# Loading plain attention units with three DMAs for both batches, and running them first

## The chip, the cores and the metric

The kernel runs on one core of a Trainium2 chip. A core has a matrix engine (TensorE, PE in the profile, with its weight loads as PEld), a vector engine (VectorE, DVE), a scalar engine (ScalarE, ACT), GpSimd (POOL) and SyncE (SP). Each engine follows its own list of instructions in order and waits on semaphores for the others. Transfers between the chip's main memory and the on-chip memory run on 16 DMA engines that all issuers share. In this kernel GpSimd issues all loads of q, k, v and nearly all weight loads; SyncE issues two early loads and all stores.

The metric is the device time of one execution in microseconds (us). The kernel before takes 175.22 us (median of 3 runs, 174.65 to 175.56).

## The reference

Attention over 8 batches, 8 heads, 576 positions and 64 dimensions, with two kinds of mask: the first four heads ("plain") look back over 32 neighbouring positions, the last four ("dilated") over 128 positions, every fourth of them. Its output, put together per token (4608 tokens x 512), goes through a soft mixture of experts: 8 experts with 4 slots each.

```python
mask_plain = (rel >= 0) & (rel < window)                      # window 32
mask_dil = (rel >= 0) & (rel < window * dilation) & (rel % dilation == 0)
scores = np.where(masks, scale * q @ k.T, -1e9)
attn = softmax(scores) @ v                                    # per batch and head
x = attn.transpose(0, 2, 1, 3).reshape(B * S, H * D)

logits = x @ phi                                              # 4608 x 32
d = softmax(logits, axis=0);  c = softmax(logits, axis=1)
slot_input = (d.T @ x).reshape(E, S_per_e, D)
slot_out[e] = np.maximum(slot_input[e] @ w1[e], 0) @ w2[e]    # w1: 512 x 1024, w2: 1024 x 512
out = c @ slot_out
```

The inputs are float32: 28.3 MB of q, k and v, 33.6 MB of weights. The output is 9.4 MB. The kernel converts to bfloat16 inside the loads.

## The kernel before

**Units.** Attention is cut into eight units, `u` = 0 to 7. A unit is one kind of head (four heads) of one pair of batches, `bp = u // 2`. `kind(u)` is 0 for plain and 1 for dilated; before the change it is `1 - u % 2`, so the units run dilated, plain, dilated, plain and so on.

**Loading a unit** (`load_unit`, L435 to L452). The stage `stg` has three slots of 96 rows by 9216 bfloat16; unit `u` uses slot `u % 3`. Rows 0 to 31 hold q, 32 to 63 k, 64 to 95 v. In the source a head has 8 stretches of 72 positions; a stretch, 72 x 64 = 4608 elements, is one row of half a slot. A dilated unit is loaded by three DMAs (one each for q, k, v), in which a row holds two neighbouring stretches. A plain unit is loaded by six: one for each of q, k, v and each batch of the pair. Batches alternate by row, and the two halves of a row are two heads (16 stretches apart). Each DMA is issued on GpSimd.

**Copies on GpSimd** (`interleave`, L598 to L610; `blocked`, L583). In a plain unit the two halves of a row must come to lie side by side before a transpose can take both. GpSimd does this with eight copies per unit, two for each of four parts `j`, viewing pairs of bfloat16 as one float32. The first part goes to scratch `hTT`, the others into slots of the stage that earlier copies have read. Dilated units need no copies.

**Stages of a unit.** `st_T` (L625) transposes a unit's 96 rows on TensorE in four parts and ScalarE writes the results to `TT` (L667), two neighbouring columns packed as one 32-bit word. `st_S` computes scores on TensorE (L685), ScalarE takes the exponential into `PT` (L692), VectorE multiplies by the mask (L700): six blocks per unit. `st_V` transposes v back (L710) and VectorE copies it to `VN` (L715): four groups. `st_P` multiplies `PT` by `VN` (L739); VectorE takes reciprocals of the sums (L748) and writes the scaled outputs to a buffer `XB` (L750): four groups. `XB` is one of five buffers, one for a batch and kind. Before the change a group's output belongs to one batch (`b = 2 * bp + bpar`), and a buffer is taken at the first of the two groups of a batch. `st_X` transposes `XB` (L767) into `XT` (L779, L780). After both kinds of a pair of batches, `st_L` computes logits (L794), their exponentials (L799), and adds the slots' inputs into `psA` (L838).

**Weights and the end.** Weight loads go out on GpSimd too (L481, L495, L870), between the unit loads, into a buffer `WD`, then into slots of the stage and into `TT` as units are done with them. After attention come the first layer of all experts (L950), the second (L1025), and the output matmuls (L1092, L1143), whose results ScalarE and VectorE scale (L1066, L1067, L1109) and SyncE stores (L1055 to L1058). The last weights arrive as two column halves, and the outputs' first part is computed and stored by halves too, so that stores of the first half go out while the second half's weights are under way. Filler matmuls (L1161) are placed in a stretch given by `FILL`.

**Order.** The order of instructions on each engine is decided before the kernel is built by a small planner, `schedule`: a list scheduler with a cost for each operation, and a key for each, from `due(u, x)` with the constants in `DUE` (a unit's pace, and offsets of each stage) and a tolerance `TOL`. GpSimd's and SyncE's operations keep the order of the program. For GpSimd that order is: unit 0's load, a constant, unit 1's load, the masks, unit 2's load; then for each unit `u`, after the transposes of `u`: weight loads, the load of unit `u + 3` into the slot that `u` has left, and the copies for unit `u + 1` if it is plain:

```python
        if u + 1 < NU and blocked(u + 1):
            interleave(u + 1)
```

The functions that the diff touches follow.

Of the kernel before, what the change touches and what calls it, by code (L numbers as in the profile page):

```python
# [18 lines left out]
SCALE = 1.0 / (D ** 0.5)  # L19
TOL, LINE, FETCH0 = 0.0806, 6.2, 193  # L20
DUE = {"pace": 8.24, "T": -11.42, "Tj": 4.19, "Te": 18.27, "S": -11.29, "Si": 0.41,
       "m": 22.09, "V": 3.07, "Vg": 3.25, "P": 6.98, "Pg": 3.6, "X": 19.47, "Xb": -72.44,
       "L": 4.86, "Lb": 20.25, "x": -24.07}
CT = 72
NU = 8
QB = 96
HALO = 32
# [29 lines left out]
class Op:  # L57
    n = 0
# [269 lines left out]
def bass_dilated_sliding_attn__then__soft_moe_slots_kernel(  # L328
# [23 lines left out]
    VNt = [sb(f"VN{i}", [128, 6, 2, 66]) for i in range(NVN)]  # L352
    XBt = [sb(f"XB{i}", [QB, 6, 256]) for i in range(NXB)]
    XTt = [sb(f"XT{i}", [128, 2, S]) for i in range(NXT)]
# [5 lines left out]
    id0 = sb("id0", [128, 128])  # L360
    ident = sb("ident", [128, 128])
    sel = sb("sel", [128, N_SLOTS])
    fold = sb("fold", [128, N_SLOTS], F32)
# [56 lines left out]
    b_mask = [Buf(), Buf()]  # L420
    b_id0, b_id, b_sel, b_fold, b_rowm, b_phist, b_phi = [Buf() for _ in range(7)]
    b_acc, b_psA, b_csum, b_rcs, b_rtok = [Buf() for _ in range(5)]
# [6 lines left out]
    def kind(u):  # L429
        return 1 - u % 2  # L430

    def load_unit(u):
        bp, ty, s = u // 2, kind(u), u % 3

        def f(g):  # L435
            res = []
            for t, src in enumerate((q, k, v)):
                if ty:
                    rows = src[2 * bp:2 * bp + 2].rearrange(
                        "b h (p c) d -> b (h p) (c d)", c=CT)[:, 32:64]  # L440
                    res.append(g.dma_start(
                        stg[32 * t:32 * t + 32, s, :],
                        rows.rearrange("b (r x) f -> r b (x f)", x=2)))
                    continue
                for bpar in range(2):
                    rows = src[2 * bp + bpar].rearrange(
                        "h (p c) d -> (h p) (c d)", c=CT)[32 * ty:32 * ty + 32]
                    res.append(g.dma_start(  # L448
                        stg[32 * t + bpar:32 * t + 32:2, s, :].rearrange("r (x f) -> r x f", x=2),
                        rows.rearrange("(x r) f -> r x f", x=2)))  # L450
            return res
        op("pool", f, w=[b_stg[s]], cost=3.5, sem=s_u[s], nbytes=96 * 2 * 4608 * 4, ndma=3 if ty else 6)  # L452

# [108 lines left out]
    for j in range(4):  # L562
        op("dve", lambda g, j=j: g.memset(rowm[32 * j:32 * j + 8, :], 1.0), w=[b_rowm], cost=0.1)
        op("dve", lambda g, j=j: g.tensor_copy(sel[32 * j:32 * j + 32, 8 * j:8 * j + 8],
                                               ident[32 * j:32 * j + 32, 32 * j:32 * j + 8]),
           r=[b_id], w=[b_sel], cost=0.1, key=1)
        op("dve", lambda g, j=j: g.tensor_copy(fold[32 * j:32 * j + 32, :],
                                               ident[32 * j:32 * j + 32, 32 * j:32 * j + 32]),
           r=[b_id], w=[b_fold], cost=0.1, key=1)
    op("dve", lambda g: g.memset(phi_pad[:], 0.0), w=[b_phi], cost=0.4, key=1)  # L570
    for hi in range(2):
# [10 lines left out]

    def blocked(u):  # L583
        return u > 0 and kind(u) == 0

# [3 lines left out]
    def il_ap(u, j, y):  # L589
        s_ = u % 3  # L590
        if j == 0:
            ap = hTT[0:96, 1152 * y:1152 * y + 1152]
# [5 lines left out]
    def interleave(u):  # L598
        s_ = u % 3
        for j in range(4):  # L600
            b_il[u, j] = Buf()
            for y in range(2):
                def f(g, j=j, y=y):
# [5 lines left out]
                op("pool", f, r=[b_stg[s_]], a=[b_il[u, j]],  # L609
                   **({"w": [b_scr]} if j == 0 and y == 0 else {}), cost=0.8, port=True)  # L610

# [13 lines left out]
    def st_T(u, j):  # L625
# [5 lines left out]
        def pe(t):  # L631
            for a in range(2):
                for kk in range(9):
                    if blocked(u):
                        i_ = t.transpose(bankb2(pt, a)[:, 96 * kk:96 * kk + 96],  # L635
                                         il_ap(u, j, a)[:, 128 * kk:128 * kk + 128],
                                         ident[0:96, 0:96])
                        continue
                    if ty:
                        c = 36 * (j // 2) + 2 * (9 * a + kk) + j % 2  # L640
                        i_ = t.transpose(bankb2(pt, a)[:, 96 * kk:96 * kk + 96],  # L641
                                         two[:, c, :], ident[0:96, 0:96])
                        continue
                    c = 18 * j + 9 * a + kk
                    for hx in range(2):
                        i_ = t.transpose(
                            bankb2(pt, a)[64 * hx:64 * hx + 64, 96 * kk:96 * kk + 96],
                            src[:, hx, c, :], ident[0:96, 0:96])
            return i_
        o = op("pe", pe, r=[b_id, b_stg[s]] +  # L650
               ([b_il[u, j]] + [b_scr] * (j == 0) if blocked(u) else []), w=[pt], alloc=[pt],
               cost=0.86 if ty == 0 and not blocked(u) else 0.75,
               mode="h" if ty == 0 and not blocked(u) else "f", n=36 if ty == 0 and not blocked(u) else 18,
               key=due(u, DUE["T"] + DUE["Tj"] * j))
# [65 lines left out]
    def st_P(u, g):  # L720
        bp, ty = u // 2, kind(u)
        bpar, h01 = g // 2, g % 2
        b = 2 * bp + bpar
        po, rv = tile(psum, 2), tile(pRV)
        vn = U[u]["v", g]
        al = [po]
        if h01 == 0:
            XB[b, ty] = tile(pXB)
            al.append(XB[b, ty])
        xb = XB[b, ty]  # L730
        pts = {(6 * g + m) // 4: U[u]["p", (6 * g + m) // 4] for m in range(6)}

        def pe(t):
            for m in range(6):
                i, x = divmod(6 * g + m, 4)
                for half in range(2):
                    o_ = 384 * half + QB * x
                    bk, po_ = (half, m) if ty == 0 else (m // 3, 3 * half + m % 3)
                    i_ = t.matmul(pair(po)[:, bk, 65 * po_:65 * po_ + 65],  # L739
# [3 lines left out]
        k0 = due(u, DUE["P"] + DUE["Pg"] * g)  # L743
        op("pe", pe, r=list(pts.values()) + [vn], w=[po], alloc=al, cost=0.46, n=12, key=k0)

        def pv():
            return pair(po)[0:QB, :, 0:390].rearrange("p x (m d) -> p x m d", d=65)
        op("dve", lambda dv: dv.reciprocal(sbt(rv)[:], pv()[:, :, :, 64]),  # L748
           r=[po], w=[rv], alloc=[rv], cost=0.15, key=k0 + 1.0)
        op("dve", lambda dv: dv.tensor_tensor(  # L750
            sbt(xb)[:].rearrange("p m (x h d) -> p h x m d", x=2, h=2)[:, h01], pv()[:, :, :, 0:64],
            sbt(rv)[:].unsqueeze(3).to_broadcast([QB, 2, 6, 64]), AluOp.mult),
           r=[po, rv], **{"w" if h01 == 0 else "a": [xb]}, cost=0.87, key=k0 + 1.2)

# [101 lines left out]
    def wpair(na, nb, s_, steps):  # L856
# [4 lines left out]
        for n, st in enumerate(steps):  # L861
# [11 lines left out]
            for b in bs:  # L873
                b.parts.append((0, 8, 0, 512, pb))
                b.ready.append(o)

    W_AFTER = {2: ["w10"], 3: ["w11"], 4: ["w12"], 5: ["w13"], 6: ["w14"]}
    for u in range(NU):
# [334 lines left out]
```

## Time and profile before

| what | value |
|---|---|
| median of 3 runs | 175.22 us (174.65 to 175.56) |
| the profiled execution | 174.82 us |
| its span, first to last instruction | 173.6 us |
| mean granted TensorE clock | 0.935 |
| PE / PEld / DVE / ACT / POOL busy | 127.1 / 98.5 / 115.3 / 94.9 / 64.3 us |
| read from main memory / written | 61.93 MB / 9.44 MB |

The profile is of one execution. Its page lists busy times of each engine; the span cut in 40 slices with busy shares in tenths (9 is 90% or more), for the DMA engines too; DMA queues; the chain of work that ended last; and the costliest groups of instructions, each with its line, engine, operation, what it writes and reads, and the idle time of the engine just before it with the engine that ended it. "L448" is line 448 of the kernel. DMA engines' shares can pass 1.00 in a short window, since a packet's time is put down as a whole. GB/s counts bytes as written: a load that converts float32 to bfloat16 reads twice as many.

### The profile page before, as it was taken

To read this page: it belongs to the slowest core of one execution; us is meant where nothing else is said; L and a number is where in the kernel's file an instruction comes from. 1 tells how busy PE (TensorE), PEld (TensorE's weight loads), DVE (VectorE), ACT (ScalarE), POOL (GpSimd) and SP (SyncE) were. 2 spreads that over 40 slices of the span, in tenths; PEclk is the share of its full clock that TensorE was granted. 3 is DMA by queue.
4 is the path that set the end of the run, shared out by engine and by line. 5 is a ranking of instruction groups with operands and counts; after the bars stand their busy time and mean duration, and the time that the engine had idled before them with its cause. 6 is when DMAs were issued, how large, how long until landed. Compare 5 with 4: busy or idle time off the path is not lost.

```text
span 173.6 us, 5093 instructions
## 1 busy us (share of the span) xinstructions
PE 127.1 (73%) x2235; PEld 98.5 (57%) x2235; DVE 115.3 (66%) x261; ACT 94.9 (55%) x145; POOL 64.3 (37%) x106
## 2 busy tenths in 40 slices
PE   0004968987889799999898789898759987699000
PEld 0004848976779588788687579576545443452000
DVE  6960059578996989978979996899540110589400
ACT  2310682878878586788788578576400110589200
POOL 7950099330696205980101762935920000000000
PEclk9999985899999999999999999999995699999955
DMA  5999999999999999999999999999999999999997
GB/s 166 286 208 193 210 232 200 215 214 216 237 208 195 216 218 210 233 220 194 215 212 219 215 215 215 215 215 217 219 204 200 212 191 197 272 382 413 436 463 311
DMA packets 10357, 41.28 MB, mean 238 GB/s; under 512 B 2016, under 2 KB 5856, under 8 KB 7008
## 3 DMA queue, kind: packets, MB, share of 16 engines
q0 software_dynamic: 7952, 30.41, 87.2%
q1 hardware_dynamic: 2384, 10.55, 15.4%
q8 instruction: 17, 0.28, 0.6%
q14 instruction: 4, 0.03, 0.0%
HBM read 61.93 MB, written 9.44 MB: 411 GB/s over the span
## 4 chain that ended last, share of the span: by engine, by line
PE 35%; DVE 24%; DMA 22%; ACT 6%; POOL 4%; issue 3%
DMA TT<-in_moe_w_dram 15%; PE ps L641 8%; DMA stg<-in_v_dram 7%; PE ps L635 7%; DVE XB L750 6%; PE ps L710 5%; DVE PT L700 5%; PE ps L685 4%; DVE WD L1066 4%; PE ps L739 3%; PE ps L794 3%; POOL TT L481 3%; PE ps L767 3%; ACT PT L692 3%; ACT TT L667 2%
## 5 line engine op out<-in xcount | busy, mean ns | idle before, releaser
L692 ACT ACTIVATE PT<-ps 128x768 bf16<-128x768 f32 x48 | 37.1, 815 | 13.1 <-PE ps L685 13.0
L667 ACT ACTIVATE TT<-ps 128x864 f32<-128x864 f32 x32 | 27.7, 898 | 17.6 <-PE ps L641 11.9
L750 DVE TENSOR_TENSOR XB<-ps,RV 96x768 bf16<-96x768 f32 x32 | 30.1, 946 | 0.5
L641 PE MATMUL ps<-ident,stg 96*128 96x96 bf16 x288 | 16.5, 224 | 15.9 <-DMA stg<-in_v_dram 15.6
L715 DVE COPY VN<-ps 128x768 bf16<-128x768 bf16 x32 | 17.1, 541 | 13.8 <-PE ps L710 13.5
L641 PEld LDWEIGHTS ps<-ident,stg 96*128 96x128 bf16 x288 | 15.3, 109 | 16.6 <-DMA stg<-in_v_dram 15.6
L739 PE MATMUL ps<-VN,PT 128*128 128x65 bf16 x384 | 17.8, 197 | 3.1 <-issue 1.4
L685 PE MATMUL ps<-TT 64*128 64x96 bf16 x384 | 15.8, 206 | 5.7 <-ACT PT L692 2.3
L710 PE MATMUL ps<-ident,TT 128*128 128x128 bf16 x192 | 16.8, 229 | 1.3 <-issue 0.6
L608 POOL COPY stg<-stg 96x576 f32<-96x576 f32 x24 | 16.8, 698 | 1.5
L739 PEld LDWEIGHTS ps<-VN,PT 128*128 128x128 bf16 x384 | 14.9, 100 | 4.1 <-issue 2.2
L685 PEld LDWEIGHTS ps<-TT 64*128 64x128 bf16 x384 | 9.7, 95 | 10.2 <-ACT PT L692 3.9
L700 DVE TENSOR_TENSOR PT<-PT,mask_d 128x768 bf16<-128x768 bf16 x24 | 15.4, 674 | 0.0
L1067 ACT ACTIVATE WD<-ps,rtok 128x256 f32<-128x256 f32 (+1 forms) x20 | 9.4, 600 | 10.2 <-PE ps L1092 10.2
L448 POOL DMA_DIRECT2D stg<-in_q_dram x8 | 4.1, 518 | 28.4 <-PE ps L641 28.4
L710 PEld LDWEIGHTS ps<-ident,TT 128*128 128x128 bf16 x192 | 11.7, 102 | 4.8 <-issue 1.3
L767 PE MATMUL ps<-ident,XB 96*128 96x96 bf16 x192 | 11.2, 207 | 1.9 <-DVE XB L750 1.6
L700 DVE TENSOR_TENSOR PT<-PT,mask_p 128x768 bf16<-128x768 bf16 x24 | 12.4, 543 | 0.1
L767 PEld LDWEIGHTS ps<-ident,XB 96*128 96x128 bf16 x192 | 9.0, 98 | 3.2 <-DVE XB L750 2.8
L780 ACT ACTIVATE XT<-ps 128x576 bf16<-128x576 bf16 x16 | 9.9, 651 | 1.8 <-PE ps L767 1.7
L635 PE MATMUL ps<-ident,stg 96*128 96x96 bf16 x216 | 10.7, 209 | 0.0
L635 PEld LDWEIGHTS ps<-ident,stg 96*128 96x128 bf16 x216 | 10.0, 99 | 0.5 <-ACT PT L692 0.2
(96 smaller groups left out, 206.5 us busy)
## 6 DMA issues: line engine op xcount, KB each, us to landing
WD<-in_moe_w_dram POOLq DMA_DIRECT2D x4, 1024.0 KB, 23.1
stg<-in_moe_w_dram POOLq DMA_DIRECT2D x3, 1024.0 KB, 29.1
out_dram<-WD SPq DMA_DIRECT2D x1, 3072.0 KB, 11.0
stg<-in_q_dram POOLq DMA_DIRECT2D x4, 576.0 KB, 17.0
stg<-in_k_dram POOLq DMA_DIRECT2D x4, 576.0 KB, 19.1
stg<-in_v_dram POOLq DMA_DIRECT2D x4, 576.0 KB, 21.5
stg<-in_q_dram POOLq DMA_DIRECT2D x8, 288.0 KB, 16.3
stg<-in_k_dram POOLq DMA_DIRECT2D x8, 288.0 KB, 18.0
```

Of the source, the lines that this page charges most:

```text
L608: return g.tensor_copy(o_, i_)
L635: i_ = t.transpose(bankb2(pt, a)[:, 96 * kk:96 * kk + 96], il_ap(u, j, a)[:, 128 * kk:128 * kk + 128], ident[0:96, 0:96])
L641: i_ = t.transpose(bankb2(pt, a)[:, 96 * kk:96 * kk + 96], two[:, c, :], ident[0:96, 0:96])
L667: return ac.activation(d, sv, ACTF.Copy)
L685: i_ = t.matmul(pair(sc)[:, hx, QB * x:QB * x + QB], win(u, 1, h01, blk_, bpar)[64 * hx:64 * hx + 64], win(u, 0, h01, blk_, bpar)[64 * hx: ...
L692: op("act", lambda ac: ac.activation(sbt(pt)[:, 0:768].rearrange("p (x n) -> p x n", x=2), pair(sc)[:, :, 0:384], ACTF.Exp, scale=SCALE), ...
L700: return dv.tensor_tensor(p_, p_, m.unsqueeze(1).to_broadcast([128, 2, 384]), AluOp.mult)
L710: i_ = t.transpose(bankb(pv)[:, 128 * m:128 * m + 128], win(u, 2, h01, m, bpar), ident[:, :])
L715: op("dve", lambda dv: dv.tensor_copy(sbt(vn)[:, :, :, 0:64], bankb(pv)[:, 0:768].rearrange("p (m x d) -> p m x d", m=6, x=2)), r=[pv], w= ...
L739: i_ = t.matmul(pair(po)[:, bk, 65 * po_:65 * po_ + 65], sbt(pts[i])[:, o_:o_ + 128], sbt(vn)[:, m, half, 0:65], start=True, stop=True)
L750: op("dve", lambda dv: dv.tensor_tensor(sbt(xb)[:].rearrange("p m (x h d) -> p h x m d", x=2, h=2)[:, h01], pv()[:, :, :, 0:64], sbt(rv)[: ...
L767: i_ = t.transpose(bankb(px)[:, QB * m:QB * m + QB], sbt(xb)[:, m, 128 * x:128 * x + 128], ident[0:QB, 0:QB])
```

## The change

The change alters how plain units are loaded and what follows from that, and the order of kinds.

- `kind(u)` becomes `u % 2`: units run plain, dilated, plain, dilated.
- A plain unit is loaded by three DMAs, one each for q, k and v. Each writes every third row (`t`, `t + 3`, ...), and the two halves of a row are now the same stretch of the two batches.
- After the copies, side by side lie the two batches, so a transpose puts one batch in partitions 0 to 63 and the other in 64 to 127. The rows are brought to the order that the later stages expect by transposing with a permutation, `perm`, in place of the identity. `perm` is built by one VectorE copy from `ident`. The two columns in a 32-bit word of `TT` are now two heads.
- A group of `st_P` of a plain unit now gives one head of each batch, so it writes two `XB` buffers with one instruction; both are taken at the first group, and the groups are kept in order. For this the five buffers become one tensor, `XBa`, and the two batches' halves of the matmul result are put in the order of the buffers' places.
- `J0` says from which part on a plain unit goes through GpSimd's copies, for the first unit and for the others. It is `(0, 0)`: unit 0, now plain, is copied whole like the others. `interleave(0)` stands before the loop, behind the loads of units 0, 1 and 2. Unit 7, now dilated, has no copies.
- `TOL` and the constants in `DUE` get new values.

```diff
-TOL, LINE, FETCH0 = 0.0806, 6.2, 193
-DUE = {"pace": 8.24, "T": -11.42, "Tj": 4.19, "Te": 18.27, "S": -11.29, "Si": 0.41,
...
+TOL, LINE, FETCH0 = 0.1176, 6.2, 193
+DUE = {"pace": 7.91, "T": -8.23, "Tj": 4.2, "Te": 0.05, "S": -27.93, "Si": 5.43,
...
+J0 = (0, 0)
...
-    XBt = [sb(f"XB{i}", [QB, 6, 256]) for i in range(NXB)]
+    XBa = sb("XB", [QB, NXB, 6, 256])
+    XBt = [XBa[:, i] for i in range(NXB)]
...
     def kind(u):
-        return 1 - u % 2
+        return u % 2
...
             for t, src in enumerate((q, k, v)):
+                rows = src[2 * bp:2 * bp + 2].rearrange("b h (p c) d -> b (h p) (c d)", c=CT)
                 if ty:
...
-                for bpar in range(2):
-                    rows = src[2 * bp + bpar].rearrange(
-                        "h (p c) d -> (h p) (c d)", c=CT)[32 * ty:32 * ty + 32]
+                else:
                     res.append(g.dma_start(
-                        stg[32 * t + bpar:32 * t + 32:2, s, :].rearrange("r (x f) -> r x f", x=2),
-                        rows.rearrange("(x r) f -> r x f", x=2)))
+                        stg[t:96:3, s, :].rearrange("r (b f) -> r b f", b=2),
+                        rows[:, 0:32].rearrange("b r f -> r b f")))
...
+    op("dve", lambda g: g.tensor_copy(
+        perm[:].rearrange("p (t r x) -> p t r x", t=3, x=2),
+        ident[0:96, 0:96].rearrange("p (x r t) -> p t r x", t=3, x=2)),
+       r=[b_id], w=[b_perm], cost=0.2, key=1)
...
-    def blocked(u):
-        return u > 0 and kind(u) == 0
+    def blocked(u, j=3):
+        return kind(u) == 0 and j >= J0[u > 0]
...
     def interleave(u):
         s_ = u % 3
-        for j in range(4):
+        for j in range(J0[u > 0], 4):
...
+                    elif blocked(u, j):
+                        in_, id_ = il_ap(u, j, a)[:, 128 * kk:128 * kk + 128], perm[:]
...
     def st_P(u, g):
...
-        b = 2 * bp + bpar
+        bs = [2 * bp + bpar] if ty else [2 * bp, 2 * bp + 1]
+        first = h01 == 0 if ty else g == 0
...
+        if first:
+            for b in bs:
+                XB[b, ty] = tile(pXB)
+                al.append(XB[b, ty])
...
-                    bk, po_ = (half, m) if ty == 0 else (m // 3, 3 * half + m % 3)
+                    bk, po_ = (half ^ (xi()[0] > xi()[1]), m) if ty == 0 else (m // 3, 3 * half + m % 3)
...
+        o = op("pe", pe, r=list(pts.values()) + [vn], w=[po], alloc=al, cost=0.46, n=12, key=k0,
+               after=[] if first else U[u]["o", bs[0]])
...
+            lo, hi = sorted(xi())
+            c = 128 * bpar + 64 * h01
+            return XBa[:, lo:hi + 1:hi - lo, :, c:c + 64]
...
+    interleave(0)
     W_AFTER = {2: ["w10"], 3: ["w11"], 4: ["w12"], 5: ["w13"], 6: ["w14"]}
```

## The prediction

> **What bounds the kernel now.** I read four views: the page's slices and queues, the landings of single loads, the waits, and the last 50 us in order of time.
>
> The page comes first: engines, slices, queues.
>
> ```profile
> span 173.6 us, 5093 instructions
> PE 127.1 (73%) x2235; PEld 98.5 (57%) x2235; DVE 115.3 (66%) x261; ACT 94.9 (55%) x145; POOL 64.3 (37%) x106
> ...
> DMA  5999999999999999999999999999999999999997
> ...
> q0 software_dynamic: 7952, 30.41, 87.2%
> ```
>
> No engine is busy throughout; the transfers are, from the second slice to the last but one. The windows (engines, clock, share of the DMA engines, GB/s written) say the same in numbers:
>
> ```profile
> 20.00:36.00 16.00, 13.61 (x243) 12.26 (x242) 10.55 (x19) 10.02 (x13) 11.31 (x19) 0.79 1.02 214
> 45.00:57.00 12.00, 10.98 (x246) 9.62 (x249) 10.05 (x24) 9.09 (x14) 10.24 (x18) 1.00 1.02 216
> 96.00:124.00 28.00, 23.87 (x488) 19.43 (x480) 25.28 (x55) 18.36 (x29) 17.62 (x26) 1.00 1.03 216
> 128.00:140.00 12.00, 10.62 (x110) 6.09 (x110) 2.54 (x9) 1.36 (x6) 0.00 (x0) 0.72 1.04 203
> 150.00:172.00 22.00, 8.77 (x44) 3.78 (x40) 10.67 (x18) 9.56 (x19) 0.00 (x0) 0.83 1.04 423
> ```
>
> The loads turn float32 into bfloat16, so 216 GB/s written is 432 read, the same pace as the stores' 423. Short dips (111 GB/s from 29 to 30 us) are made good by peaks beside them: the 16 us around them average 214. So the transfers' sum is the bound, and compute matters only where it lets the queue run dry.
>
> How far is the queue from dry? After the first unit, loads land 13 to 34 us after issue, though the bytes of a unit take 8.3. These lines are answers for single moments of issue: the two v loads of plain units 1, 5 and 7 (the time is the median of the two) and, third, the v load of dilated unit 6.
>
> ```profile
> stg<-in_v_dram POOLq DMA_DIRECT2D x2, 288.0 KB, 17.0
> ...
> stg<-in_v_dram POOLq DMA_DIRECT2D x2, 288.0 KB, 22.1
> ...
> stg<-in_v_dram POOLq DMA_DIRECT2D x1, 576.0 KB, 26.1
> ...
> stg<-in_v_dram POOLq DMA_DIRECT2D x2, 288.0 KB, 25.9
> ```
>
> The issue waits for compute, as the waits show (GpSimd for the transposes that free a stage):
>
> ```profile
> POOL stg L448 <- PE ps L641: 28.4, 3, 10.8
> ```
>
> Yet a load issued at 67 us still had some 20 us of transfers ahead of it. The chain that ended last hangs on a transfer too:
>
> ```profile
> 121.59 4.33 POOL TT L481 x6
> 125.93 25.25 DMA TT<-in_moe_w_dram
> ```
>
> In time order TensorE has 7 + 2 filler matmuls (1.69 and 0.60 us) before it waits for the last weights:
>
> ```profile
> 142.05 1.69 PE L1161 MATMUL ps<-wrm 128*128 128x512 bf16 x7
> ...
> 146.83 0.29 PE L1025 MATMUL ps<-TT,hTT 128*32 128x256 bf16 x4 [0.50 <-DMA TT<-in_moe_w_dram]
> ```
>
> With that wait and two issue gaps of 0.40 and 0.42 us beside the second filler the room is some 3.6 us: compute may end so much later before the first store moves.
>
> **The change part by part.** The sum is made against the profiled execution: 174.82 us, span 173.6 and 1.2 around it, 0.40 below the median of 175.22.
>
> *Three DMAs in place of six in each plain unit.* GpSimd issues 12 fewer, at 0.51 us (L448: 8 x 0.518, 0.508, 0.519): 6.2 us less, all of it beside a full queue, so nothing on the path. Were the queue dry, 1.5 us per unit would count. The bytes and the 9,216-byte rows stay; what may change is how fast they flow. By landings: plain unit 1 took 8.06 us (15.5 to 23.56), unit 3 8.4 (34.5 to 42.9), unit 7 8.43 (87.93 to 96.36); unit 5 took 9.15, but the weights behind it 4.1 where such a piece takes 4.9 to 5.2, so 8.3 is its fair share. Dilated units, three DMAs already, took 8.39, 8.2, 8.2. Mean 8.30 against 8.26: 4 x 0.04 = 0.16, and I take -0.2. Ends: no plain unit slower than the best, 8.06, gains 4 x 0.24 = 1.0; all as slow as unit 5 at face value loses 4 x 0.85 = 3.4. I stay near the dilated rows, since the new load has their number of DMAs and their 32 destination rows.
>
> *Plain units first, unit 0 behind copies.* Unit 0 lands at 15.5 as now (same bytes, three DMAs at 1.4 to 3.0 us). Then 8 copies at 663 to 878 ns: 5.3 to 7.0 us on GpSimd, the first transposes after two. The last transposes end at some 22 to 24 us against 21.4 now (72 in 5.84 us), so first scores and issue of unit 3 come 0.6 to 2.5 us later. Moved behind these copies on GpSimd's queue are half of w10 (issued at 10.3 now, then at 21 to 23) and unit 3's three DMAs, 1.5 us. Cover: unit 2's bytes last until 31.95, a margin of 8 us. Without it each microsecond would count once. VectorE sits idle from 12.3 to 23.6 anyway, so the copies disturb nobody there.
>
> *Unit 1 without copies.* Its transposes start near 23.6, on landing, where now they wait for GpSimd until 29.3; unit 4's load goes out near 28 instead of 34.4. Earlier behind a queue: nothing.
>
> *Unit 7 without copies.* Now it lands at 96.4, is copied until 102.7, and its last transposes end at 107.4. Dilated, they can start at 96.4. VectorE has 25.3 us of work in the 28 from 96 to 124, so it sets how much of 6 us remains: 1 to 5 us earlier at the end of attention. It lengthens the 3.6 us of room and gains nothing, since the last weights still land at 151.
>
> *Outputs for both batches.* A plain unit takes two XB buffers at its first group, of five; pairs hold four until the logits of the first batch are done. Its XB line writes the same 96 x 768 elements (946 ns). Transposes of XB wait for all four groups, not two. Queued behind on VectorE are masks and V copies, and TensorE waits for those. No row shows the stall: between 0 and, three times, a whole pause such as the longest of TensorE on XB now (1.3 us), some 4 us. Near the low end, since units arrive 13.3 us apart and need about 12.5 us of VectorE. It lies within 3.6 plus 1 to 5 us of room: 0. If that cover goes, the excess counts.
>
> *The permutation* is one VectorE copy of 96 elements per row, between the sel copy (0.17 us) and the slowest fold (1.07), before 12.3 us; unit 0 lands at 15.5. Nothing. *New due times* only reorder, within the same room.
>
> Sum: -0.2, so 174.6 on the profiled execution's scale and 175.0 as a median. What is late next: still the last weights, then 22 us of stores.
>
> **The rivals.**
>
> *A, the loads flow faster.* The two weights w15 and w16 (2,048 KB, 128 rows) landed 9.6 us after unit 7, 218 GB/s, against 213 for 1.77 MB in 8.30. Plain loads now write 32 neighbouring partitions with six DMAs; then each writes every third of 96. At the weights' pace a unit takes 8.10, a gain of 4 x 0.20 = 0.8; the fastest row, unit 0, whose q, k and v land 2.6 us apart (7.8 for a unit), would give 2.0. I take 1.2: 174.0 as a median. Against it: dilated loads write neighbours too, with three DMAs, and are no faster.
> [...]
>
> *B, a slow clock at the end (slower).* The granted clock was 0.5 from 131 to 137 us, and groups of matmuls 512 wide then followed each other by 0.43 us, where at full clock near 144 us it was 0.22. If attention ends 1 to 5 us earlier, TensorE stands waiting for weights before 140, where the filler starts, and such a stretch may fall on 146 to 153: the twelve output matmuls of each half (1.48 us) take 2.9, and first stores come 0.7 us later in each half, with the store queue empty between. +1.4: 176.6. It decides once the stores of the first half (1.57 MB, 3.7 us) drain before those of the second are issued; at 153 to 155 us the rate already sags to 374 and 356 GB/s. Against it: the filler and 26 matmuls lie between.
> [...]
>
> *C, compute late.* XB pairs and GpSimd's copies cost more than the 5 to 8 us of room: at 10 us late, +2 to +3, 177.5. For it: VectorE is busy 88% from 24 to 124. Against it: unit 7's saved copies.
>
> *D, uneven destinations.* Three-apart rows keep some transfer engine behind, as in unit 5: 4 x 0.85, 178.2 (the change fails at what it does).
>
> **How the numbers follow.** Transfers bind everywhere, so no change is likeliest, 0.40; A 0.32; B 0.13; C 0.10; D 0.05. Half a per cent, 0.88 us, is about what a measurement here can tell. Of A, 0.27 lies beyond that bound (its own runs from 0.8 to 2.0), and of the likeliest 0.03 below and 0.02 above it. So faster: 0.27 + 0.03 = 0.30; slower: 0.13 + 0.10 + 0.05 + 0.02 = 0.30; same: 0.40. The likeliest case by itself runs from 174.3 to 175.8. For the range I add nearly all of A, down to 173.5, and B with part of C, up to 177.0; outside stay D, the rest of C and a tail of A.
>
> **What would show it.** Right: DMA share at 9 in all slices but the first and last, unit landings 8.2 to 8.4 us apart from the load before, the chain ending on TT weights that land near 151, 12 fewer issues and 6 us less on GpSimd, unit 0's transposes ending at 22 to 24, stores from 148.5. A: plain landings at 8.1 or less and the last weights before 150. B: clock 0.5 within 146 to 153 and a DMA slice below 9 there. C: TT loads issued after 126 us, no filler, no DMA wait at 146. D: a late second batch of rows in each plain unit. I would be wrong above all if a queue of 12 to 20 us ran dry somewhere, which I see no place for.

## The result and the profile after

Each kernel ran 22 times beside the other: 174.65 us before (174.25 to 175.83) and 174.26 us after (173.97 to 174.66). The medians differ by 0.39 us. The ratio is 0.9971, with a 95% interval of 0.9961 to 0.9981: 0.29% or half a microsecond faster, inside the half per cent that the prediction had called the bound of a measurement, though these 22 runs resolve it. (The three runs shown before had their median at 175.22, so the 175.0 predicted lies 0.7 above what was measured.) Here and below a ratio leaves out runs over 1.5% above the fastest of their kernel, while medians are over all runs. The profiled execution took 174.12 us, 0.70 less than that of before, and its span is shorter by the same 0.7.

The page of the changed kernel, with engines, slices, packets and the loads' queue:

```profile
span 172.9 us, 5074 instructions
PE 127.8 (74%) x2232; PEld 97.9 (57%) x2233; DVE 112.6 (65%) x261; ACT 95.9 (55%) x146; POOL 57.0 (33%) x94
...
DMA  5999999999999999999999999999999999999997
...
DMA packets 10165, 41.28 MB, mean 239 GB/s; under 512 B 1824, under 2 KB 5664, under 8 KB 6816
...
q0 software_dynamic: 7760, 30.41, 87.2%
```

The transfers still fill every slice but the first and the last. Bytes are the same. The loads' queue has 192 packets fewer (7952 before), and the packets under 512 B fell by the same 192 (2016 before): 12 DMAs fewer with 16 small packets each. GpSimd lost 12 instructions and 7.3 us.

The windows say how fast it flows. First before, then after, for the 100 us in which all units arrive, and for the end:

```profile
24.00:124.00 100.00, 88.58 (x1831) 75.27 (x1830) 87.61 (x180) 73.01 (x105) 49.76 (x78) 0.97 1.02 214
```

```profile
24.00:124.00 100.00, 90.05 (x1852) 74.86 (x1850) 86.45 (x179) 74.56 (x107) 41.78 (x65) 1.00 1.03 216
128.00:140.00 12.00, 11.20 (x133) 6.56 (x134) 2.02 (x8) 1.36 (x6) 0.00 (x0) 0.86 1.04 206
150.00:172.00 22.00, 9.03 (x47) 4.11 (x44) 10.57 (x18) 9.24 (x18) 0.00 (x0) 0.81 1.01 416
```

The engines are full in both, with shares of 1.02 and 1.03, and 216 GB/s are written in place of 214. The same bytes are therefore through a little earlier. Where that shows is the landing of the last weight load. The trace has one completion of it for each of the sixteen DMA engines: the mean moved from 150.16 to 149.60 us, the last of them from 151.18 to 150.48. From the mean landing to the last store's landing it is 23.4 us before and 23.2 after, and from the last engine's 22.4 in both, so the stores pass the gain on.

The chain that ended last after the change, from the issue of the last loads of weights, and then SyncE's first store, before and after:

```profile
118.28 2.04 POOL TT L480 x3
120.32 25.47 DMA TT<-in_moe_w_dram
...
146.72 2.66 PE ps L1107 x12
```

```profile
148.65 2.58 SPq L1058 DMA_DIRECT2D out_dram<-WD  x4
```

```profile
147.80 2.93 SPq L1073 DMA_DIRECT2D out_dram<-WD  x4
```

The chain again waits for a transfer, but for an earlier one. Before, it waited for the right half of the last weights, until 151.18. Now it waits for the left half, which lands at 120.32 + 25.47 = 145.79, against 146.78 before, and then follows TensorE. The last weights land at 150.48 and the matmuls that need them start at 150.53, right behind others, so both paths end together. The first store goes out 0.85 us earlier.

TensorE in order of time, from the end of attention (the fold) to the first output matmuls:

```profile
128.29 2.07 PE L943 MATMUL ps<-fold,psA_sb 128*128 128x32 f32 x8 [0.80 <-DVE psA_sb L936]
...
139.40 1.25 PE L1176 MATMUL ps<-wrm 128*128 128x512 bf16 x5
...
143.92 0.61 PE L1176 MATMUL ps<-wrm 128*128 128x512 bf16 x2
...
145.83 0.29 PE L1040 MATMUL ps<-TT,hTT 128*32 128x256 bf16 x4 [1.05 <-DMA TT<-in_moe_w_dram]
146.72 2.66 PE L1107 MATMUL ps<-so_sb,expT 128*128 128x256 bf16 x12 [0.59 <-DVE so_sb L1081]
```

The fold ran at 129.59 before, so attention ends 1.3 us earlier. Filler and a wait for the weights are there as before. The twelve output matmuls took 2.66 us where they took 1.48: the granted clock was 0.55 from 146.5 to 150 us, 1.00 in the same stretch before. More on that below.

### The profile page after: what moved, and what is told of

Read it like the earlier page. It is cut to its first block, busy times and chain, and to the rows that moved or that the text cites. A ratio compares the mean times of both kernels' runs of the same rounds, so it can differ in the third digit from the quotient of the medians.

```text
span 172.9 us, 5074 instructions
## 1 busy us (share of the span) xinstructions
PE 127.8 (74%) x2232; PEld 97.9 (57%) x2233; DVE 112.6 (65%) x261; ACT 95.9 (55%) x146; POOL 57.0 (33%) x94
## 4 chain that ended last, share of the span: by engine, by line
DMA 37%; PE 26%; DVE 20%; ACT 4%; POOL 4%; issue 2%
DMA stg<-in_v_dram 22%; DMA TT<-in_moe_w_dram 15%; PE ps L648 11%; DVE XB L764 5%; DVE WD L1081 4%; DVE PT L700 3%; DVE VN L715 3%; PE ps L685 3%; PE ps L710 2%; PE ps L744 2%; PE ps L781 2%; ACT TT L667 2%; PE ps L1107 2%; PE ps L808 2%; DVE stg L1081 2%
## 5 line engine op out<-in xcount | busy, mean ns | idle before, releaser
L692 ACT ACTIVATE PT<-ps 128x768 bf16<-128x768 f32 x48 | 36.5, 813 | 9.7 <-PE ps L685 9.5
L667 ACT ACTIVATE TT<-ps 128x864 f32<-128x864 f32 x32 | 28.3, 897 | 20.5 <-PE ps L648 20.0
L648 PE MATMUL ps<-perm,hTT 96*128 96x96 bf16 x72 | 4.4, 225 | 16.0 <-POOL hTT L611 16.0
L744 PEld LDWEIGHTS ps<-VN,PT 128*128 128x128 bf16 x384 | 14.5, 98 | 3.0 <-DVE PT L700 0.7
L648 PE MATMUL ps<-ident,stg 96*128 96x96 bf16 x288 | 15.1, 208 | 1.3 <-DVE PT L700 0.7
L648 PEld LDWEIGHTS ps<-ident,stg 96*128 96x128 bf16 x288 | 13.2, 99 | 2.2 <-DVE PT L700 0.8
L700 DVE TENSOR_TENSOR PT<-PT,mask_d 128x768 bf16<-128x768 bf16 x24 | 13.2, 582 | 0.0
L648 PEld LDWEIGHTS ps<-perm,hTT 96*128 96x128 bf16 x72 | 3.8, 108 | 16.2 <-POOL hTT L611 16.0
L648 PE MATMUL ps<-perm,stg 96*128 96x96 bf16 x216 | 12.6, 225 | 0.2 <-ACT TT L667 0.2
L794 ACT ACTIVATE XT<-ps 128x576 bf16<-128x576 bf16 x17 | 10.6, 651 | 2.4 <-PE ps L781 2.4
L648 PEld LDWEIGHTS ps<-perm,stg 96*128 96x128 bf16 x216 | 11.4, 108 | 0.5 <-ACT TT L667 0.3
```

Of the source, the lines that this page charges most:

```text
L648: i_ = t.transpose(bankb2(pt, a)[:, 96 * kk:96 * kk + 96], in_, id_)
L667: return ac.activation(d, sv, ACTF.Copy)
L692: op("act", lambda ac: ac.activation(sbt(pt)[:, 0:768].rearrange("p (x n) -> p x n", x=2), pair(sc)[:, :, 0:384], ACTF.Exp, scale=SCALE), ...
L700: return dv.tensor_tensor(p_, p_, m.unsqueeze(1).to_broadcast([128, 2, 384]), AluOp.mult)
L744: i_ = t.matmul(pair(po)[:, bk, 65 * po_:65 * po_ + 65], sbt(pts[i])[:, o_:o_ + 128], sbt(vn)[:, m, half, 0:65], start=True, stop=True)
L794: return en.activation(d, s_, ACTF.Copy)
```

## The experiments

Every explanation has to answer where half a microsecond came from: fewer DMAs, rows spread over the partitions, or compute that is earlier or later by the new order. The runs went in three groups, each beside the kernel before on its own chip; a ratio is to that. Landings are those of the last weight load, mean over the engines and last engine, of one profiled execution each. Two executions of the changed kernel itself gave 149.60 / 150.48 and 149.56 / 150.31.

| kernel | DMAs of the units | median us | ratio (95%) | landing, mean / last | first store | span |
|---|---|---|---|---|---|---|
| before | 36 | 174.65 | 1 | 150.16 / 151.18 | 148.65 | 173.6 |
| after | 24 | 174.26 | 0.9971 (0.9961 to 0.9981) | 149.60 / 150.48 | 147.80 | 172.9 |
| after, second time | 24 | 174.14 | 0.9962 (0.9943 to 0.9981) | 149.56 / 150.31 | 147.59 | 172.9 |
| plain with six | 36 | 174.35 | 0.9959 (0.9930 to 0.9988) | 149.93 / 150.61 | 147.81 | 173.1 |
| plain with three, neighbours | 24 | 174.25 | 0.9955 (0.9920 to 0.9990) | 149.77 / 150.59 | 147.81 | 173.0 |
| plain with six, neighbours | 36 | 174.70 | 1.0001 (0.9978 to 1.0024) | 150.20 / 151.29 | 148.48 | 174.1 |
| all units with six | 48 | 174.48 | 0.9969 (0.9945 to 0.9993) | 150.15 / 150.87 | 148.15 | 173.5 |
| dilated spread too | 24 | 174.06, 174.23 | 0.9933 (0.9905 to 0.9962), 0.9955 (0.9928 to 0.9981) | 149.59 / 150.21, 149.72 / 150.59 | 147.55, 147.79 | 172.7, 173.0 |
| unit 0 not copied | 24 | 174.76 | 0.9991 (0.9964 to 1.0018) | 149.54 / 150.94 | 148.14 | 173.5 |
| unit 7 without q | 23 | 171.55 | 0.9777 (0.9717 to 0.9837) | 146.92 / 147.66 | 145.93 | 170.6 |
| no masks | 24 | 174.97 | 0.9994 (0.9959 to 1.0028) | 149.65 / 150.50 | 150.22 | 174.9 |
| load alone, old order | 24 | 179.89 | 1.0247 (1.0192 to 1.0301) | 149.56 / 150.21 | 153.27 | 177.9 |
| new order, old due times | 24 | 200.03 | 1.1357 (1.1280 to 1.1434) | 161.55 / 162.54 | 175.16 | 199.8 |

The kernel before had medians of 174.97, 174.99 and 174.75 us in the three groups, so ratios compare better across groups than medians do. The first group holds plain with six, plain with three neighbours, all units with six, and the load alone; the second holds dilated spread (its first time), unit 7 without q, no masks, and the old due times; the rest are the third, the only one with the changed kernel in it. There were 12 runs of each, but 6 of the last two rows and 4 of unit 7 without q.

### Do the transfers bind? Unit 7 without its q load

```diff
-            for t, src in enumerate((q, k, v)):
+            for t, src in list(enumerate((q, k, v)))[u == 7:]:
```

> The changed kernel without the load of q in unit 7 (its scores then use what lies in the stage): 0.59 MB written, 1.18 MB read less of 71.4 MB. If transfers bind: the time falls by what such a DMA takes, 2.7 us, to 171.5, ratio 0.982. If compute binds anywhere behind unit 7: less than half of that.

Measured: 171.55 us, 2.6 to 2.7 less than the changed kernel, and the last weights landed 2.68 us earlier by the mean.

```profile
span 170.6 us, 5073 instructions
```

```profile
145.93 2.58 SPq L1073 DMA_DIRECT2D out_dram<-WD  x4
```

```profile
128.64 2.08 PE L943 MATMUL ps<-fold,psA_sb 128*128 128x32 f32 x8 [0.80 <-DVE psA_sb L936]
```

What was taken out of the queue came off the time in full. Attention ended no earlier than in the changed kernel (fold at 128.64 against 128.29), so it was not compute that gave way. The sum of the transfers is the bound, as the prediction had it.

### Does compute bind? No mask multiplications

```diff
-        def mk(dv):
-            m = mask[ty][:, m0:m0 + 4, :].rearrange("p m x -> p (m x)")
...
-        op("dve", mk, r=[b_mask[ty]], w=[pt], cost=0.47, key=k0 + DUE["m"], port=True)
```

> The changed kernel without the 48 multiplications by the masks (the scores are not masked): VectorE loses 25.6 us of its 112.6. If transfers bind (theories 1 and 2): as the changed kernel, 0.997, with attention ending earlier and TensorE waiting for the last weights. If compute is part of the bound (theory 3): faster by microseconds, below 0.985.

Measured: 174.97 us, ratio 0.9994, with runs from 174.16 to 176.16. The profiled execution is the longest of them.

```profile
PE 129.7 (74%) x2230; PEld 100.8 (58%) x2231; DVE 93.2 (53%) x217; ACT 93.6 (54%) x142; POOL 56.3 (32%) x94
```

```profile
134.01 2.08 PE L936 MATMUL ps<-fold,psA_sb 128*128 128x32 f32 x8 [0.80 <-DVE psA_sb L929]
```

```profile
150.22 2.58 SPq L1066 DMA_DIRECT2D out_dram<-WD  x4
```

VectorE works 19.4 us less than in the changed kernel, and nothing is faster, as it should be if VectorE's work does not set the time. The edit did not take out that work alone, though. Without the masks the planner lays out another order, attention ended 5.7 us later in that execution (fold at 134.01 against 128.29), and the first store came 2.42 us later, although the weights landed at 149.65 as before. This measures the room, in one execution: 5.7 - 2.4 = 3.3 us may be lost before stores move.

### The number of DMAs: plain units with six again, rows still spread

```diff
-                    res.append(g.dma_start(
-                        stg[t:96:3, s, :].rearrange("r (b f) -> r b f", b=2),
-                        rows[:, 0:32].rearrange("b r f -> r b f")))
+                    for b in range(2):
+                        res.append(g.dma_start(
+                            stg[t:96:3, s, 4608 * b:4608 * b + 4608], rows[b, 0:32]))
```

> The changed kernel, but each plain unit loaded by six DMAs again (one per tensor and batch, same destination rows, same row sizes). Theory 1 (fewer DMAs: what was won is the completions of 12 DMAs, some 0.04 us each): back to the time of before, ratio 1.000. Theory 2 (destination: rows spread over 96 partitions let the transfer engines run more evenly) and theory 3 (order of work: units, due times, the end of attention) both say as the changed kernel, 0.997.

Measured: ratio 0.9959. By time nothing is lost that the interval shows; by landings 0.34 us by the mean (149.93 against 149.56 and 149.60).

```profile
DMA packets 10357, 41.28 MB, mean 238 GB/s; under 512 B 2016, under 2 KB 5856, under 8 KB 7008
```

The packets are exactly those of before again, and GpSimd was busy 62.4 us, 5.4 more than with three. So 5.4 us of issues on GpSimd cost nothing in time that these runs resolve. If the 0.34 us are due to the twelve DMAs, one costs 28 ns of the transfers' time.

### The rows: plain units with three, but in neighbouring partitions

```diff
-                        stg[t:96:3, s, :].rearrange("r (b f) -> r b f", b=2),
+                        stg[32 * t:32 * t + 32, s, :].rearrange("r (b f) -> r b f", b=2),
...
-        ident[0:96, 0:96].rearrange("p (x r t) -> p t r x", t=3, x=2)),
+        ident[0:96, 0:96].rearrange("p (t x r) -> p t r x", t=3, x=2)),
```

> The changed kernel, still three DMAs in a plain unit, but q, k and v go to 32 neighbouring partitions each, with the permutation matrix changed to suit. Theory 2 (destination): the gain goes, ratio 1.000, and the last transfer engine of a plain load ends over 1 us behind the middle one, as in unit 0 before. Theories 1 (fewer DMAs) and 3 (order): 0.997.

Measured: ratio 0.9955; landing 149.77, 0.17 to 0.21 us later. Spreading the rows alone is not where the gain comes from either. The lag that was expected does show in unit 0: the last engine lands 1.2 us behind the middle one in each of its three loads, against 0.2 to 0.3 in the changed kernel. In the later plain units the changed kernel has 0.5 to 1.6 us as well.

### Both undone: six DMAs into neighbouring partitions

The edits of the last two together, with the destination `stg[32 * t:32 * t + 32, s, 4608 * b:4608 * b + 4608]`; the order, the copies and the due times stay those of the changed kernel.

> The changed kernel with six DMAs in plain units and neighbouring destination rows, both at once, that is with the old number and the old neighbourhood in the new order of units and new due times. If the number (0.24 to 0.32 us by the landings so far) and the spread (0.17) add up: last load at 150.0 to 150.1 and the whole gain gone, 0.25 to 0.3% over the control. If only the number counts: as the kernel with six DMAs and spread rows, 149.9. If neither: as the control.

Measured: ratio 1.0001, against 0.9962 for the changed kernel in the same group. The whole gain is gone.

```profile
span 174.1 us, 5086 instructions
```

```profile
146.65 0.29 PE L1040 MATMUL ps<-TT,hTT 128*32 128x256 bf16 x4 [1.56 <-DMA TT<-in_moe_w_dram]
```

TensorE waits for the left half of the weights until 146.65, where the changed kernel had it at 145.83 and the kernel before at 146.83. The landings are those of before, 150.20 against 150.16. So by time the new order with its due times gives nothing, within 0.2%, when the load's gain is taken away. By landings the two parts add up: 0.34 + 0.19 is close to the 0.62 of both. By time each alone costs nothing and both together 0.4%, with intervals of 0.2 to 0.35% each; and the profiled execution of this last kernel lay 0.63 us above its own median, so its landing may be late by some of that.

How the two share the gain, the packets in the traces show in part. This table adds up their times in the loads' queue, in us for each of the 16 engines; other weight packets, 17.4 us, are the same in all:

| kernel | packets of 4 bytes, 16 for each DMA | plain units' data | dilated units' data | weights in packets of 8 KB | whole queue |
|---|---|---|---|---|---|
| before | 1.58 | 33.65 | 33.20 | 65.50 | 151.37 |
| after | 1.28 | 33.63 | 33.15 | 65.23 | 150.73 |
| after, second time | 1.31 | 33.67 | 33.12 | 65.18 | 150.73 |
| plain with six | 1.54 | 33.63 | 33.19 | 65.14 | 150.95 |
| plain with three, neighbours | 1.31 | 33.77 | 33.16 | 65.14 | 150.83 |
| plain with six, neighbours | 1.69 | 33.95 | 33.20 | 65.17 | 151.47 |
| all units with six | 1.82 | 33.61 | 33.14 | 65.24 | 151.27 |

The number of DMAs shows in the small packets: twelve more cost 0.25 us, another twelve 0.28. A block of 32 neighbouring partitions costs the plain units' data 0.12 us with three DMAs and 0.30 with six. But the kernel before wrote every other row of such a block, and its plain data took no longer than the changed kernel's. So of the 0.64 us between before and after, 0.29 is the number of DMAs, and the rows are no part of it in these executions. The last 0.29 us lies in weights that the change does not touch: from 130 us on their packets took 649 ns on the mean before, and 625 to 638 in the other runs whose queue stayed full. Why is open; it may belong to this one execution of the kernel before, which took 0.70 us more than that of after where the medians differ by 0.39.

### All units with six

The plain load of the six-DMA kernel, and each dilated load split by batch as well:

```diff
-                    res.append(g.dma_start(
-                        stg[32 * t:32 * t + 32, s, :],
-                        rows[:, 32:64].rearrange("b (r x) f -> r b (x f)", x=2)))
+                    for b in range(2):
+                        res.append(g.dma_start(
+                            stg[32 * t + b:32 * t + 32:2, s, :],
+                            rows[b, 32:64].rearrange("(r x) f -> r (x f)", x=2)))
```

> The changed kernel with six DMAs in every unit, plain and dilated, each half the rows or half the row, with descriptors of the same size: 24 DMAs more than the changed kernel. Theory 1 (fewer DMAs): twice the loss of the kernel with six in plain units alone, ratio 1.003, some 1.0 us over the changed kernel. Theories 2 and 3: 0.997; a small loss below 0.2 us would fit them too.

Measured: ratio 0.9969, landing 150.15.

```profile
DMA packets 10549, 41.28 MB, mean 238 GB/s; under 512 B 2208, under 2 KB 6048, under 8 KB 7200
```

Another 12 DMAs and another 192 small packets put the landing back by 0.22 us, 18 ns for each DMA, beside the 28 of the first twelve. In time it is 0.1% against the kernel with 36, within the intervals. The mean landing is that of before, yet the ratio is that of the changed kernel (0.9971). What differs from before is the last engine, 150.87 against 151.18. Within one execution the end goes with the last of the sixteen rather than with their mean: leaving out the three kernels whose compute ends late (no masks and the last two rows), the span ends 22.4 to 22.9 us after the last engine's landing and 23.1 to 24.0 after the mean.

### Dilated rows spread too

```diff
-                        stg[32 * t:32 * t + 32, s, :],
+                        stg[t:96:3, s, :],
...
+        permd[:].rearrange("p (t r) -> p t r", t=3),
+        ident[0:96, 0:96].rearrange("p (r t) -> p t r", t=3)),
```

This second permutation takes the identity's place for dilated units. The expectation of the first run:

> The changed kernel, with the dilated units too written to every third row of 96 (and transposed with a permutation of their own); number and size of DMAs as in the changed kernel. If spread destinations are part of the gain (theory 2; in single profiles the neighbours version's last load landed 0.17 us later), the dilated units give as much again: the last load lands some 0.2 us earlier than in the changed kernel, ratio 0.996. If only the number of DMAs counts (theory 1) or only the order (theory 3): as the changed kernel, 0.997.

and of its repeat, beside the changed kernel run a second time:

> The version with all units written to every third row once more, beside the control. Its first profile had the last load at 149.59, where the changed kernel had 149.60, so by the landings it should equal the control within 0.1%; by its first times, 174.06, it should be 0.1 to 0.3% faster.

> The changed kernel itself, as a control beside the next three on one chip: ratio 0.997 to the kernel before, last load landing at a mean of 149.6 us over the transfer engines.

Measured: 0.9933 the first time, which looked like another 0.3%; the second time 0.9955 beside 0.9962 for the unchanged version. Landings of 149.59 and 149.72 say the same: no gain. The first ratio was scatter between groups.

### Unit 0 without copies

```diff
-J0 = (0, 0)
+J0 = (4, 0)
```

> The changed kernel with unit 0 transposed straight from the stage, by 144 half transposes, and not behind GpSimd's eight copies. If the copies are hidden behind a full queue, as the prediction has it: as the control within 0.1%, though unit 0's transposes end 2 us or so earlier or later. If the start counts: a change of 0.5 us or more.

Measured: ratio 0.9991, against 0.9962 for the changed kernel in the same group: 0.6 us slower, not faster. The copies were hidden, and the half of w10 and the load of unit 3 that wait behind them cost nothing: the mean landing is the same without them, 149.54. But the last engine landed at 150.94, and the chain now ends on that one:

```profile
span 173.5 us, 5199 instructions
...
q8 instruction: 18, 0.29, 0.6%
```

```profile
123.83 27.11 DMA TT<-in_moe_w_dram
150.94 0.04 issue
```

Without copies unit 0 needs 144 half transposes for 72, so the program has 125 instructions more, and one more fetch of instructions over the DMA engines (18 against 17). A fetch keeps one of the sixteen engines for some 0.95 us; the last one fell at 148.8 us instead of 143.6, and in the end one engine lay 1.5 us behind the middle one. That the fetch is what held it back fits the numbers, but no run took the fetch alone away.

### The load alone, in the old order with the old due times

```diff
     def kind(u):
-        return u % 2
+        return 1 - u % 2
...
-    interleave(0)
+    if blocked(0):
+        interleave(0)
```

`TOL` and `DUE` have the values of before.

> The loading change alone: three DMAs and rows by both batches as in the changed kernel, outputs to two buffers, but dilated units first and the due times of the kernel before, so unit 0 is not copied and unit 7 is. Theories 1 (fewer DMAs) and 2 (destination): the whole gain, ratio 0.997. Theory 3 (order, due times, unit 7 without copies): none of it, 1.000.

Measured: 179.89 us, ratio 1.0247, although the weights landed as early as in the changed kernel (149.56).

```profile
124.44 2.10 PE L781 MATMUL ps<-ident,XB 96*128 96x96 bf16 x24 [2.56 <-DVE XB L764]
126.34 4.04 PE L808 MATMUL ps<-XT,phi_pad 128*128 128x192 bf16 x16
...
137.14 2.08 PE L944 MATMUL ps<-fold,psA_sb 128*128 128x32 f32 x8 [0.80 <-DVE psA_sb L937]
```

```profile
153.27 2.58 SPq L1074 DMA_DIRECT2D out_dram<-WD  x4
```

Here the last unit is plain. Its groups belong to both batches, so the transposes of `XB` (24 in one go) and the logits of both batches (16 in one go) come only after the fourth group; before the change the first batch's went ahead. The fold runs at 137.14: 7.6 us later than before, 8.9 later than in the changed kernel. The first store is 5.5 us later than there, so the room is 8.9 - 5.5 = 3.4 us, close to the 3.3 above. The due times here were chosen for the old load, so the 7.6 us are the price with those, and no run parts what the layout costs from what the due times add.

### The new order with the old due times

```diff
-TOL, LINE, FETCH0 = 0.1176, 6.2, 193
+TOL, LINE, FETCH0 = 0.0806, 6.2, 193
```

and `DUE` with the values of before.

> The changed kernel with the tolerance and due times of the kernel before. Theories 1 and 2: transfers as in the changed kernel, and 0.997 as long as attention ends in time for the last weights; the loading change in the old order and with the old times ended late and took 1.025. If the old times alone are to blame for that, this one takes about 1.02 too; if the order of units is, 0.997.

Measured: 200.03 us, ratio 1.1357. The page's slices of the DMA engines, the waits, and two windows:

```profile
DMA  6999999999999999999999996299399940069998
```

```profile
POOL stg L884 <- PE ps L648: 31.3, 1, 31.3
POOL stg L480 <- PE ps L648: 21.8, 1, 21.8
```

```profile
124.00:140.00 16.00, 14.19 (x248) 11.06 (x246) 11.93 (x26) 9.14 (x16) 6.71 (x12) 0.84 0.70 129
160.00:176.00 16.00, 14.89 (x182) 8.79 (x182) 3.62 (x11) 2.83 (x11) 0.00 (x0) 0.79 0.12 17
```

The queue ran dry. GpSimd stood 31.3 and 21.8 us before loads of weights whose slot of the stage was still waiting for TensorE's transposes (L648); from 124 to 140 us the engines were busy 70%, from 160 to 176 us 12%, where the changed kernel keeps them at 1.01 from 150 us to its end. The due times put the transposes of a unit late, and these free the slots. The old order with the new due times was not run.

## Why the prediction was right, and where it was wrong

**The bound.** The likeliest case, no change within half a per cent because the transfers bind, is what came. Taking out one load shows the bound (2.6 to 2.7 us of time for 2.68 of transfers, with attention ending no earlier). Taking out the masks made nothing faster, though in another order of work.

**Three DMAs in place of six** is the term that was mis-sized: -0.2 us against -0.5 in time and -0.56 in the mean landing. The step was "Mean 8.30 against 8.26: 4 x 0.04 = 0.16", differences of landings within one execution. There, plain units alone ran from 8.06 to 9.15, and a difference of 0.04 from such rows has no meaning. Taken from the last landing of each load in the same trace, with 8.3 again for unit 5, the rows give 8.25 for plain units and 8.30 for dilated ones, which would be no gain at all: that the sign came out right is luck. The reason given, fewer DMAs, was sound, and the small packets price it: 0.25 to 0.29 us for the twelve. By landings the runs put 0.34 us on the twelve DMAs and 0.19 on the rows; by time they show only that undoing both loses the gain.

**Rival A** had the direction right and the size too large, -0.5 and not -1.2, and its cause is not what the packets show: a data packet of a plain unit took 701.0 ns before and 700.6 after. Nor did its signs come: units 2, 4 and 6, now plain, landed 8.2 to 8.3 us after the load before them, not 8.1 or less, and the last engine at 150.48, not before 150. Where the rows go shows in the runs only in part: in the plain loads a block of neighbours costs 0.19 us by landings with three DMAs (149.77 against 149.56 and 149.60), 0.27 (150.20 against 149.93) and 0.4% of the time with six (the 0.4% from two groups); spreading the dilated rows gave nothing in two runs (149.59 and 149.72 against 149.56 and 149.60). Why placement matters in the one and not in the other stays open.

**Unit 0 behind copies: 0.** Right. These are GpSimd's lines in order of time, then TensorE's:

```profile
14.54 1.38 POOL L611 COPY hTT<-stg 96x576 f32<-96x576 f32 x2 [5.54 <-DMA stg<-in_v_dram]
15.99 4.29 POOL L611 COPY stg<-stg 96x576 f32<-96x576 f32 x6
20.23 0.56 POOL L480 DMA_DIRECT2D WD<-in_moe_w_dram  x1
22.25 0.51 POOL L443 DMA_DIRECT2D stg<-in_q_dram  x1 [1.47 <-PE ps L648]
```

```profile
15.98 1.62 PE L648 MATMUL ps<-perm,hTT 96*128 96x96 bf16 x18 [15.98 <-POOL hTT L611]
17.43 4.52 PE L648 MATMUL ps<-perm,stg 96*128 96x96 bf16 x54
```

The copies take 5.7 us (5.3 to 7.0 was worked out), the transposes end at 21.95 (22 to 24), half of w10 goes out at 20.23 (21 to 23), unit 3's load at 22.25. These come early because unit 0 landed at 14.5 us and not at 15.5 as the text had it. All of it stays in front of the queue, and the kernel without these copies lands its weights no earlier by the mean.

**Unit 1 without copies: 0.** Right in effect. Unit 4's load went out at 31.64 where the text had 28 and the kernel before 34.4; behind the queue its v landed at 55.90 against 56.27 before, 0.4 us earlier for an issue 2.8 us earlier.

**Unit 7 without copies** let attention end 1.3 us earlier, at the lower end of "1 to 5", and gained nothing, as said. The room was to be 3.6 plus 1 to 5; it is 3.3 to 3.4, since the left half of the weights lands 1.0 us earlier too: 3.6 + 1.3 - 1.0 = 3.9. The text had not taken the earlier landing off; the other 0.5 us stays open.

**Outputs for both batches: 0** was right for this kernel only, and for a reason that the text did not see. The bounds, 0 to 4 us, priced a stall of TensorE on `XB`. What the kernel with the load alone shows is both batches' transposes and logits behind the last group of the last unit, and an end of attention 7.6 us later, above the upper bound; the old due times may have a share in it, which no run parts. Here the last unit is dilated, and attention ends 1.3 us earlier than before. What was costed as "unit 7 without copies" may be above all this; no run tells the two apart.

**"New due times only reorder, within the same room"** was wrong. With the old ones the new order takes 200.03 us. They decide when stage slots come free, and the statement that a queue of 12 to 20 us had no place to run dry held only for orders that free slots in time.

**Rival B** took place and cost little. Windows of engines, clock, share and GB/s in the changed kernel:

```profile
144.00:146.00 2.00, 0.95 (x10) 0.24 (x10) 0.00 (x0) 0.00 (x0) 0.00 (x0) 1.00 1.45 193
146.50:150.00 3.50, 3.28 (x19) 2.11 (x20) 2.35 (x5) 2.58 (x6) 0.00 (x0) 0.55 1.36 234
```

TensorE was busy 0.95 of the 2 us from 144 on, where in the kernel before it was busy for all 2.00; then the granted clock was 0.55, and the twelve output matmuls took 2.66 us for 1.48. But the first store needs only the first few of them: from the start of the left half's last matmuls to the store's issue 1.97 us went by, 1.82 before. The price is 0.15 us rather than 0.7 in each half, because the second half's last matmuls need weights that land at 150.48 anyway. What makes the clock fall is not shown. In both executions of the changed kernel it was 0.50 from 147 to 150 us, after a wait of 1.05 us in a stretch half idle; with unit 0 not copied TensorE waited 1.05 us at the same place, and its twelve output matmuls took 1.48 us.

**Rival C** is the kernel with the load alone, at 179.9. Its condition, compute later by more than the room, was right; the changed order avoids it. **Rival D**, an engine left behind by rows three apart, was not seen: at the last load the last engine is 0.9 us behind the mean after, 1.0 before.

## What to carry to other kernels

Where a queue of transfers binds, price a change of loads by the landing of the last load over all engines of DMA, and mistrust differences between units of one execution that are smaller than their own scatter. A change of layout in the last stage's unit may cost many times its instructions (here the fold came 7.6 us later, with due times chosen for the old load), since it decides what can go ahead of the final group; look at what the last unit waits for, and in which order the kinds run. Constants of a planner belong to an order: with those of another one the queue that hides everything can run dry, as at 200.03 us here.

## What the runs showed of the hardware

- An extra DMA in a queue that is full all the time brought 16 packets of 4 bytes, of 18 to 21 ns each on the mean in these traces. Twelve DMAs so took 0.25 to 0.4 us of each engine's time, and put the landing of the last load back by 0.34 us and, for the next twelve, by 0.22; two executions of one kernel differ by 0.04 to 0.13. By time this is at the edge of what was resolved.
- The wait for the last load ended with its slowest engine: the chain has that load until 151.18 before the change and until 150.94 with unit 0 not copied, in both the last engine's landing, 1.0 and 1.4 us after the mean. With the same mean landing (149.54 and 149.56) a last engine at 150.94 in place of 150.31 went with 0.6 us more. Fetches of instructions, about 0.95 us on one engine each, are a candidate for what makes an engine late; this is argued, not shown.
- No version that does all the work beat the changed kernel by more than the intervals.
